# A fused attention and mixture kernel: the bias stage's pools stacked in another order

## The chip, the cores and the metric

The kernel runs on one core of one Trainium2 chip, in one launch. The metric is device time in microseconds (us): the median of repeated executions. Beside it stands one profiled execution, from which all rows below come. The engines are named as in the profile: PE (matrix multiplies), PEld (its weight loads), DVE, ACT, POOL (the three elementwise engines) and SP, which here issues every DMA (SPq is its DMA queue).

## The reference

Three layers follow each other. Attention has 4 batches, 8 heads, 576 positions of width 64, and a learned relative bias:

```python
x = (log1p(|i - j|) / log1p(max(i, 1)))[..., None]
bias = relu(x @ w1 + b1) @ w2                      # 576 x 576 x 8 heads, hidden width 32
attn = softmax(q @ k.T / 8 + bias.transpose(2, 0, 1))
x = (attn @ v)                                     # to 2304 tokens x 512
h = x @ w_in;  x = (max(h, 0) + alpha * min(h, 0)) @ w_out          # width 2048
logits = x @ phi                                   # 32 slots, 8 experts of 4
y = softmax(logits, over slots) @ experts(softmax(logits, over tokens).T @ x)
```

The bias is the same for all batches. It depends on `i` only through a scale and on `i - j`, so every row of it is a piecewise linear function.

## The kernel before, in words

**Stages.** `bias_phase` computes the bias and stores it in a DRAM tensor `W`. `Attention.run` follows, then `Moe.run` (the two dense layers and the routing) and `Experts.run`. All instructions are recorded once; a scheduler then orders each engine's instructions by a simulated timeline, apart from those that `keep_in_program_order` holds (attention from its second pair on, the late stores of the bias stage, and the preparation of the next layer's inputs among them).

**The bias stage.** For each of nine distances `k` (0 to 8) it makes 16 masks, each on DVE, ACT or POOL, in a ring of 40 (`mask`, pool `b_mask`). `unit(k, c)` multiplies masks by weights on PE into `acc` (PSUM); DVE turns `acc` into bias rows through `tmp` (L189, L190), and POOL writes their mirror image (L198) into the same tile `rows`. When a tile of rows is complete, `flush` stores it to `W` (L203, eight heads). For four of them, `rows2_2`, `rows0_2`, `rows1_3` and `rows0_3` (the number of the column block, then of the chunk), only heads 0 and 1 are stored at once; the stores of heads 2 to 7, two DMAs a tile, are put in a list `late` and issued after all else of the stage, in that order. They are the eight **late stores**, and the two of `rows0_3` are the last.

**Pools.** A tile pool is a stretch of each partition's SBUF. Pools of the left side are stacked upwards, those of `side="right"` downwards from the top, each in the order in which it is opened. The bias stage opens four on the right: `b_late` (tags b, c, d, g of the row tiles), `b_rows` (the other row tiles), `b_const` (inputs, weights, the two `tmp`) and `b_mask`. When the stage ends they are closed, and attention's and the next layer's pools grow from the left into the same bytes: `m_keep`, `m_x0`, `m_x1`, `a_z` (the scores with bias `z`, their minimum `m`, the exponentials `e`, four buffers each), `a_out`, `a_g` (four transposed tiles `g`) and `a_bias1` (the bias tile `nb` of odd head pairs). A tile waits for everything that used its bytes before, a DMA that reads them included (`reuse_waits="tile"`).

**Attention.** 16 pairs (head pair, batch) of nine tiles: `scores` (L379, PE, two PSUM buffers `s`), `shift` (L397, DVE: adds the bias `nb`, finds the minimum), `weights` (L416, ACT: exponential), `transposes` (L433, PE), `gather` (L457, one half on ACT, one on DVE, into `g`), `pv` (L472, PE). `split` (L345, L348, POOL) makes the two-part operands of a later pair. Results go to DRAM (`xT<-xo`, and the sums `rs<-rt`), and from step 8 on are loaded again (`vv<-rs`, `vv<-xT`) for the next layer's input, which DVE multiplies at L604.

**SP.** One queue, in order: an SP instruction that waits holds up all behind it. The bias tile of head pair 0, `nb`, is loaded from `W` in pieces (L310) between the last stores; behind the late stores come `early` (L622, weights of the next layer) and the `nb` of head pair 1, whose first load waits for the late stores.

Of the kernel before, what the change touches and what calls it, by code (L numbers as in the profile page):

```python
# [14 lines left out]
ALU = mybir.AluOpType  # L15
# [12 lines left out]
SLOTS = 32  # L28
# [14 lines left out]
LATE, EARLY = "bcdg", "aefmn"  # L43
# [30 lines left out]
def bias_phase(tc, ident, W, cpack, lcol, prow, xmain, xtail, att):  # L74


    nc = tc.nc
    with ExitStack() as ctx:

        def pool(name, bufs=1):  # L80
            return ctx.enter_context(tc.tile_pool(name=name, bufs=bufs, reuse_waits="tile", side="right"))

        fps = {tag: p for p, tags in ((pool("b_late"), LATE), (pool("b_rows"), EARLY)) for tag in tags}
        cp = pool("b_const")
        mp = pool("b_mask")
        ap_ = ctx.enter_context(tc.tile_pool(name="b_acc", bufs=ACC, space=PSUM, reuse_waits="tile"))

        cp_t = cp.tile([P, 14], F32, name="cp_t")
# [1039 lines left out]
def kernel(  # L1128
    ctx, tc, qk, v_l, cpack, w_l, alpha, phi, mw1, mw2, lcol, prow, xmain, xtail, scon, out
):  # L1130
    nc = tc.nc
# [5 lines left out]
    ident = const.tile([P, P], F32, name="ident")  # L1137
# [7 lines left out]
        for n, b in (("a_raw", 2), ("a_v", 3), ("a_split", 2))  # L1145
    )
    bias_phase(tc, ident, W, cpack, lcol, prow, xmain, xtail, att)

    kp = ctx.enter_context(tc.tile_pool(name="m_keep", bufs=1, reuse_waits="tile"))
    x0 = ctx.enter_context(tc.tile_pool(name="m_x0", bufs=1, reuse_waits="tile"))  # L1150
    x1 = ctx.enter_context(tc.tile_pool(name="m_x1", bufs=1, reuse_waits="tile"))
    moe = Moe(tc, ident, xT, rs, w_l, None, x0, x1)
    moe.load_alpha(alpha)
    moe.x_alloc(0)
    moe.early = x1.tile([P, 3, 1024], F32, tag="x", name="early")
    moe.idr = kp.tile([P, P], F32R, name="idr")
    nc.gpsimd.tensor_scalar(moe.idr, ident, 1.0, 1.0, ALU.mult, ALU.mult)
    moe.id4 = kp.tile([P, SLOTS], F32, name="id4")
    for k in range(4):
        q = slice(SLOTS * k, SLOTS * k + SLOTS)  # L1160
        nc.gpsimd.tensor_scalar(moe.id4[q], ident[q, q], 1.0, 1.0, ALU.mult, ALU.mult)
    set0 = att.sets[0]

    def take_stage():
# [28 lines left out]
    def at(step, f, *args):  # L1193
        extra.setdefault(step, []).append(lambda: f(*args))

    for n in range(3):
        at(3, moe.half_load, n)
    at(XONE, moe.x_alloc, 1)
# [153 lines left out]
```

## Time and profile before

| | us |
|---|---|
| median of 3 runs | 836.94 (835.46 to 837.0) |
| profiled execution | 837.26 |
| its span on the core | 835.4 |
| PE busy in the span | 772.3 (92%) |
| DVE, ACT, POOL busy | 551.8, 489.4, 332.9 |

The span is what the trace covers; 1.9 us of the execution lie around it. In the rows below a line of a timeline gives the start, the duration, engine, source line, operation, tiles written and read, the count of merged instructions, and in brackets the idle time of that engine just before and what ended it. A line of windows gives for a stretch the busy time of each engine (and instructions), the granted clock of PE as a share of full speed, the mean busy share of the DMA engines and GB/s.

### The profile page before, as it was taken

Reading aid. Unit: us, or ns where it says so; the run is one execution under the profiler, and the core shown is the slowest. Engines: PE = TensorE matmul, PEld = TensorE weight load, DVE = VectorE, ACT = ScalarE, POOL = GpSimd, SP = SyncE. Lnnn points to the kernel's source line nnn. Section 1 sums busy time; section 2 is a strip of 40 time slices with the busy share of each in tenths; the row PEclk is TensorE's granted clock in tenths of the full one; section 3 lists DMA queues with packets and bytes.
Section 4 is the critical chain, followed back from the end, with each engine's and each line's share of the span. In section 5 each row is a group of like instructions: output and inputs, shape, how many; then the busy total and the mean of one; then the engine's idle time right before and its main releaser. Section 6 shows DMA issues by size and latency. Waiting matters only on the chain.

```text
span 835.4 us, 18819 instructions
## 1 busy us (share of the span) xinstructions
PE 772.3 (92%) x7444; PEld 636.0 (76%) x7444; DVE 551.8 (66%) x1058; ACT 489.4 (59%) x1066; POOL 332.9 (40%) x423
## 2 busy tenths in 40 slices
PE   6766698999999999999999999999999999999894
PEld 5766566777767776898899888889888898988341
DVE  8766578888889886999533855575666555465202
ACT  8742467787778785434445665666566656655102
POOL 7965143555465511314312363445345233251100
PEclk9999599999999999999999999999999999999898
DMA  6799994863937211665200200050000004337996
GB/s 209 183 218 201 213 230 163 211 189 120 252 109 254 87 59 59 212 207 209 62 0 1 71 7 1 9 185 10 1 29 1 0 19 163 122 101 272 410 400 230
DMA packets 59784, 114.46 MB, mean 137 GB/s; under 512 B 10672, under 2 KB 38192, under 8 KB 57904
## 3 DMA queue, kind: packets, MB, share of 16 engines
q1 hardware_dynamic: 59696, 113.26, 44.6%
q8 instruction: 58, 0.95, 0.5%
q14 instruction: 30, 0.25, 0.1%
HBM read 91.95 MB, written 21.29 MB: 136 GB/s over the span
## 4 chain that ended last, share of the span: by engine, by line
PE 43%; DMA 4%; DVE 3%; ACT 1%; issue 1%; SPq 0%; DVEq 0%; ACTq 0%
PE ys L730 18%; PE h L697 18%; DMA ep<-in_mw_dram 2%; PE hps L1084 2%; DMA rb<-rs 1%; PE lp L789 1%; PE sp L849 0%; PE sp L848 0%; DVE vv L604 0%; DVE g L708 0%; PE tl L836 0%; DVE x L610 0%; DVE gr L718 0%; DMA vv<-xT 0%; PE tc L898 0%
## 5 line engine op out<-in xcount | busy, mean ns | idle before, releaser
L708 DVE SCALAR_TENSOR_TENSOR g<-g,nal 128x384 f32<-128x384 f32 x96 | 72.2, 752 | 77.9 <-ACT g L707 77.7
L416 ACT ACTIVATE e<-z,m 128x576 f32<-128x576 f32 x144 | 110.3, 766 | 3.8 <-DVE m L397 3.0
L397 DVE CUSTOM_DVE_ANT_0 z<-s,nb 128x576 f32<-128x576 f32 x144 | 103.3, 750 | 10.5 <-PE s L379 4.8
L716 ACT ACTIVATE gr<-g 128x384 fp32r<-128x384 f32 x95 | 49.9, 525 | 93.8 <-DVE g L708 91.6
L433 PEld LDWEIGHTS t<-ident,e 64*128 64x128 f32 x1440 | 68.3, 142 | 45.3 <-ACT g L457 12.5
L472 PE MATMUL o<-g,v 128*64 128x256 f32 (+1 forms) x640 | 94.7, 418 | 0.0
L433 PE MATMUL t<-ident,e 64*128 64x64 f32 x1440 | 81.7, 232 | 12.3 <-ACT g L457 9.6
L457 ACT ACTIVATE g<-t 128x320 f32<-128x320 f32 x144 | 62.1, 431 | 52.7 <-PE t L433 42.2
L457 DVE COPY g<-t 128x320 f32<-128x320 f32 x144 | 69.4, 485 | 28.2 <-PE t L433 23.3
L165 PE MATMUL acc<-wp,mask 128*128 128x64 bf16 (+1 forms) x1680 | 57.2, 198 | 22.4 <-issue 14.8
L705 ACT ACTIVATE g<-h 128x384 f32<-128x384 f32 x96 | 46.6, 487 | 46.4 <-PE h L697 45.8
L165 PEld LDWEIGHTS <-mask 128*128 128x128 bf16 (+1 forms) x1680 | 54.9, 103 | 24.5 <-issue 17.4
L718 DVE TENSOR_TENSOR gr<-g,gr 128x384 fp32r<-128x384 f32 x79 | 52.7, 668 | 31.1 <-ACT gr L716 29.9
L379 PE MATMUL s<-kh,qh 64*128 64x288 f32 x320 | 60.3, 346 | 7.3 <-DVE rows L190 5.4
L718 POOL TENSOR_TENSOR gr<-g,gr 128x384 fp32r<-128x384 f32 x16 | 19.3, 1207 | 117.7 <-ACT gr L716 117.7
L345 POOL TENSOR_SCALAR qh<-raw 128x608 fp32r<-128x608 f32 x32 | 21.8, 699 | 104.1 <-PE s L379 100.6
L146 ACT ACTIVATE mask<-pr,wb 128x576 bf16<-128x576 f16 (+4 forms) x81 | 47.1, 666 | 22.3 <-PE acc L165 22.2
L472 PEld LDWEIGHTS o<-g,v 128*64 128x64 f32 x640 | 41.2, 137 | 24.6 <-ACT g L457 0.5
L379 PE MATMUL s<-kl,qh 64*128 64x288 f32 x320 | 53.5, 304 | 0.0
L379 PE MATMUL s<-kh,ql 64*128 64x288 f32 x320 | 53.4, 304 | 0.0
L348 POOL TENSOR_TENSOR ql<-raw,qh 128x304 fp32r<-128x304 f32 x64 | 53.0, 860 | 0.0
L707 ACT ACTIVATE g<-h 128x384 f32<-128x384 f32 x96 | 46.6, 485 | 0.0
(1008 smaller groups left out, 2058.4 us busy)
## 6 DMA issues: line engine op xcount, KB each, us to landing
ep<-in_mw_dram SPq DMA_DIRECT2D x30, 512.0 KB
raw<-in_qk_dram SPq DMA_DIRECT2D x16, 896.0 KB
stage<-in_w_dram SPq DMA_DIRECT2D x14, 1024.0 KB
nb<-W SPq DMA_DIRECT2D x12, 576.0 KB
v<-in_v_l_dram SPq DMA_DIRECT2D x16, 320.0 KB
pre<-in_mw_dram SPq DMA_DIRECT2D x10, 512.0 KB
ex<-in_mw_dram SPq DMA_DIRECT2D x9, 512.0 KB
em<-in_mw_dram SPq DMA_DIRECT2D x8, 512.0 KB
```

Source lines behind the costliest of these rows:

```text
L165: nc.tensor.matmul(dst[:, u // 8, :, :, 4 * (u % 8) : 4 * (u % 8) + 4], mask[:, (16 * k + u) % RING, cols], wp[:, part], start=part == 0, ...
L348: self.nc.gpsimd.tensor_tensor(st[x, 1][:, c], src[:, c], st[x, 0][:, c].bitcast(F32), ALU.subtract)
L379: nc.tensor.matmul(s[:, hf, :288], st["q", a][d, o : o + P], st["k", b][d, 288 * h : 288 * h + 288], start=n_ == 0, stop=n_ == len(seq) - 1,),
L397: nc.vector.tensor_tensor_reduce(out=z.rearrange("p (a b) -> p a b", a=2), in0=s[:, :, :288], in1=self.nb[st["hp"]][:, self.SLOT[t]].rearr ...
L416: self.pin(i, nc.scalar.activation(e, z, AF.Exp, bias=m, scale=-1.0, accum_out=acc))
L433: self.pin(i, nc.tensor.transpose(tp[r][:, c], e[q, k0 : k0 + P], self.ident[q, q]))
L457: self.pin(i, nc.vector.tensor_copy(dst, src) if r else nc.scalar.activation(dst, src, AF.Copy))
L472: nc.tensor.matmul(o[64 * h : 64 * h + 64, :n], st["v"][:, h, c], g[:, c, :n], start=c == 0, stop=c == 4),
L697: nc.tensor.matmul(h, w_[:, c * P : (c + 1) * P], x_[:, c], start=c == 0 and n_ == 0, stop=c == NC - 1 and n_ == 2,)
L708: nc.vector.scalar_tensor_tensor(g, neg, self.nal[:, f : f + 1], g, ALU.mult, ALU.add)
L718: eng.tensor_tensor(gl, g, gh.bitcast(F32), ALU.subtract)
L730: i = self.nc.tensor.matmul(self.ys[blk][t], g_[:, t * P : (t + 1) * P], w_[:, 512:], start=f == 0 and n_ == 0, stop=f == NF - 1 and n_ == 2,)
```

## The change

It opens `b_const` and `b_mask` first and `b_late` and `b_rows` after them, and puts three small constants of the next layer, which were recorded right behind the bias stage, into a function that is recorded at step 16 of attention.

```diff
-        fps = {tag: p for p, tags in ((pool("b_late"), LATE), (pool("b_rows"), EARLY)) for tag in tags}
+
         cp = pool("b_const")
         mp = pool("b_mask")
+        fps = {tag: p for p, tags in ((pool("b_late"), LATE), (pool("b_rows"), EARLY)) for tag in tags}
...
-    moe.load_alpha(alpha)
     moe.x_alloc(0)
     moe.early = x1.tile([P, 3, 1024], F32, tag="x", name="early")
     moe.idr = kp.tile([P, P], F32R, name="idr")
-    nc.gpsimd.tensor_scalar(moe.idr, ident, 1.0, 1.0, ALU.mult, ALU.mult)
     moe.id4 = kp.tile([P, SLOTS], F32, name="id4")
-    for k in range(4):
-        q = slice(SLOTS * k, SLOTS * k + SLOTS)
-        nc.gpsimd.tensor_scalar(moe.id4[q], ident[q, q], 1.0, 1.0, ALU.mult, ALU.mult)
+
+    def constants():
+        moe.load_alpha(alpha)
+        nc.gpsimd.tensor_scalar(moe.idr, ident, 1.0, 1.0, ALU.mult, ALU.mult)
+        for k in range(4):
+            q = slice(SLOTS * k, SLOTS * k + SLOTS)
+            nc.gpsimd.tensor_scalar(moe.id4[q], ident[q, q], 1.0, 1.0, ALU.mult, ALU.mult)
+
...
+    at(16, constants)
```

`load_alpha` is a DMA (`nal`) and a POOL instruction that reads it. The pools' sizes follow from their tiles: `b_mask` 46,080 bytes a partition, `b_const` 17,184, `b_late` 36,864, `b_rows` 32,768. Together they take bytes 45,760 to 178,656 in both kernels. What attention's tiles lie on then is:

| tiles (bytes) | before, on | after, on |
|---|---|---|
| `m_keep`, `m_x0` (37,760 to 89,664) | `b_mask` | `b_rows`, then `b_late` |
| `early` in `m_x1` (89,664 to 101,952) | `b_mask`, `b_const` | `b_late` |
| `z` (101,952 to 111,168) | `b_const`; the last buffer also `rows3_2` | `rows0_3`; the last bytes `rows2_2` |
| `m`, `e` (111,168 to 120,512) | `rows3_2`, `rows4_2` | `rows2_2`, then `b_mask` |
| `a_out`, `a_g` (120,512 to 149,952) | `rows1_1`, `rows0_1`, `rows4_1`, `rows0_2` | `b_mask` |
| `a_bias1` (149,952 to 170,688) | `b_late` | `b_mask`, `b_const` |

The first place where instructions differ in what they wait for is DVE at the end of the bias stage. The rows give the line, the operation, what it writes and reads (with a number that tells buffers apart), the shape, and the semaphores it waits for: `DMAHW0` to `DMAHW7` count DMAs, the others are engines; `ISA` is the instruction of `shift`. Before:

```order
L190 TENSOR_TENSOR rows_3_2139<-tmp_0_2140,acc_0_2090 128x2x8x32 [waits DMAHW7_49,DMAHW1_49,Pool_49]
L190 TENSOR_TENSOR rows_3_2139<-tmp_0_2201,acc_0_2152 128x2x8x32 [waits DVE_49]
L397 ISA z_0_2292,m_0_2293<-s_0_2285,nb_1662 128x576 [waits DMAHW3_49,DMAHW6_49,DMAHW2_49,PE_49]
L397 ISA m_0_2293 128x1
L397 ISA z_1_2304,m_1_2305<-s_1_2297,nb_1662 128x576 [waits DVE_49,PE_49]
L397 ISA m_1_2305 128x1
L397 ISA z_2_2316,m_2_2317<-s_2_2309,nb_1662 128x576 [waits DMAHW5_49,DMAHW7_49,DVE_49,PE_49]
```

And after:

```order
L191 TENSOR_TENSOR rows_3_2139<-tmp_0_2140,acc_0_2090 128x2x8x32 [waits DMAHW7_49,DMAHW1_49,Pool_49]
L191 TENSOR_TENSOR rows_3_2139<-tmp_0_2201,acc_0_2152 128x2x8x32 [waits DVE_49]
L398 ISA z_0_2284,m_0_2285<-s_0_2277,nb_1662 128x576 [waits DMAHW4_49,DMAHW3_49,DMAHW5_49,DMAHW2_49,DMAHW6_49,DMAHW1_49,DMAHW7_49,PE_49,Pool_49]
L398 ISA m_0_2285 128x1
L398 ISA z_1_2296,m_1_2297<-s_1_2289,nb_1662 128x576 [waits PE_49]
L398 ISA m_1_2297 128x1
L398 ISA z_2_2308,m_2_2309<-s_2_2301,nb_1662 128x576 [waits PE_49]
```

`rows_3_2139` is `rows0_3`. In the built program the counts that the first shift waits for on `DMAHW4` and `DMAHW5` are those of the two late stores of `rows0_3`, and on `DMAHW6` and `DMAHW7` those of `rows2_2`; before, it waits for two pieces of `nb` and a store of `rows3_2`.

The second place is SP, from the last stores of heads 0 and 1 on. Before:

```order
L203 DMA W<-rows_3_1956 64x2x128
L585 DMA nal<-in_alpha_dram 128x16
L203 DMA W<-rows_2_1720 64x2x128
L310 DMA nb_1662<-W 64x2x576
L203 DMA W<-rows_2_1539 64x2x192
...
L203 DMA W<-rows_3_2139 64x6x128 x2
L622 DMA early<-in_w_dram 128x1024 x3
L310 DMA nb_3044<-W 64x4x576 x4
L310 DMA nb_3044<-W 64x576 x2
L330 DMA raw_3051<-in_qk_dram 128x1792
L484 DMA xT<-xo_0_2616 128x256
```

And after:

```order
L204 DMA W<-rows_3_1956 64x2x128
L204 DMA W<-rows_2_1720 64x2x128
L311 DMA nb_1662<-W 64x2x576 x3
L204 DMA W<-rows_2_1539 64x2x192
...
L204 DMA W<-rows_3_2139 64x6x128 x2
L311 DMA nb_3036<-W 64x576 x2
L311 DMA nb_3036<-W 64x4x576
L623 DMA early<-in_w_dram 128x1024 x3
L311 DMA nb_3036<-W 64x4x576 x3
L586 DMA nal<-in_alpha_dram 128x16
L331 DMA raw_3043<-in_qk_dram 128x1792
L485 DMA xT<-xo_0_2608 128x256
```

`nal` has moved from ahead of the late stores to behind the second bias tile; the eight late stores keep their order, and the first large load of the second bias tile now stands ahead of `early`.

On POOL `nal` stood ahead of the mirror images of `rows0_3`; now it stands behind them, right ahead of the split of pair 2. The five copies of the identity stand two mirror images earlier.

## Rows read from the trace of the kernel before

**Rows 1.** The page: busy tenths and granted clock in 40 slices of 20.9 us.

```profile
PE   6766698999999999999999999999999999999894
PEclk9999599999999999999999999999999999999898
```

**Rows 2.** Windows: busy us of each engine, PE clock, DMA share, GB/s.

```profile
80.00:90.00 10.00, 3.80 (x30) 3.13 (x32) 4.06 (x9) 2.91 (x5) 3.10 (x9) 0.59 0.86 204
90.00:100.00 10.00, 6.03 (x51) 5.45 (x49) 4.79 (x14) 3.18 (x8) 0.00 (x0) 0.50 0.99 241
100.00:110.00 10.00, 9.76 (x102) 7.37 (x104) 5.50 (x15) 6.38 (x18) 6.68 (x9) 0.72 1.03 233
110.00:120.00 10.00, 9.53 (x127) 6.54 (x124) 7.59 (x21) 6.70 (x19) 1.17 (x2) 1.00 1.06 214
130.00:140.00 10.00, 8.16 (x88) 5.87 (x88) 7.20 (x18) 5.63 (x15) 7.29 (x9) 0.83 0.59 203
```

**Rows 3.** Timeline of DVE: start, us, operation, [idle before, what ended it].

```profile
86.05 0.76 DVE L397 CUSTOM_DVE_ANT_0 z<-s,nb 128x576 f32<-128x576 f32 x1 [0.67 <-PE s L379]
...
89.55 0.76 DVE L397 CUSTOM_DVE_ANT_0 z<-s,nb 128x576 f32<-128x576 f32 x1 [2.01 <-DMA nb<-W]
...
93.74 0.76 DVE L397 CUSTOM_DVE_ANT_0 z<-s,nb 128x576 f32<-128x576 f32 x1 [2.11 <-DMA nb<-W]
...
99.61 0.49 DVE L457 COPY g<-t 128x320 f32<-128x320 f32 x1 [1.62 <-DMA W<-rows]
```

**Rows 4.** Timeline of ACT at the start of attention.

```profile
86.88 1.28 ACT L416 ACT_TABLE_LOAD   x1 [11.93 <-DVE m L397]
...
99.75 0.44 ACT L457 ACTIVATE g<-t 128x320 f32<-128x320 f32 x1 [4.01 <-DMA W<-rows]
```

**Rows 5.** Timeline of SP's DMA issues.

```profile
81.72 0.92 SPq L585 DMA_DIRECT2D nal<-in_alpha_dram  x1
82.74 0.60 SPq L203 DMA_DIRECT2D W<-rows  x1
...
84.86 0.59 SPq L310 DMA_DIRECT2D nb<-W  x1
...
91.56 7.08 SPq L203 DMA_DIRECT2D W<-rows  x8
98.69 2.23 SPq L622 DMA_DIRECT2D early<-in_w_dram  x3
104.23 4.20 SPq L310 DMA_DIRECT2D nb<-W  x6
```

**Rows 6.** Line L203, 92 to 100: durations in ns, first and last start.

```profile
L203 SPq DMA_DIRECT2D W<-rows x8: 597/798/1217, 91.6 to 98.0; - x8
```

**Rows 7.** Line L310, 101 to 104.3: SP's waits for semaphores.

```profile
L310 SPq EVENT_SEMAPHORE  x2: 28/28/28, 103.9 to 104.2; - x2
```

**Rows 8.** Timeline of PE: transposes of tiles 2 and 6, first scores of pair 2.

```profile
100.24 0.47 PE L433 MATMUL t<-ident,e 64*128 64x64 f32 x2 [2.44 <-ACT g L457]
...
107.85 0.28 PE L433 MATMUL t<-ident,e 64*128 64x64 f32 x2
...
119.94 0.38 PE L379 MATMUL s<-kh,qh 64*128 64x288 f32 x1
```

**Rows 9.** Timeline of POOL: `nal`, then the split of pair 2, first and last.

```profile
84.61 0.20 POOL L586 TENSOR_SCALAR nal<-nal 128x16 f32<-128x16 f32 x1 [2.51 <-DMA nal<-in_alpha_dram]
...
101.70 1.37 POOL L345 TENSOR_SCALAR qh<-raw 128x608 fp32r<-128x608 f32 x2 [15.63 <-PE s L379]
...
106.81 1.57 POOL L348 TENSOR_TENSOR kl<-raw,kh 128x288 fp32r<-128x288 f32 x2
```

**Rows 10.** Who SP waited for, 119 to 123: us in total, times, longest.

```profile
SPq L501 <- DMA nb<-W: 3.1, 1, 3.1
```

**Rows 11.** Timeline of SP: the last store of pair 0's sums.

```profile
122.62 0.21 SPq L501 DMA_DIRECT2D rs<-rt  x1
```

**Rows 12.** Timeline of DVE at the first input of the next layer.

```profile
133.97 0.95 DVE L604 TENSOR_TENSOR vv<-vv 128x384 f32<-128x384 f32 x1 [2.80 <-DMA vv<-xT]
```

## The prediction

> **What bounds the kernel now.** I read the page's slices first, then the windows around the place where they break, then the timelines of each engine there, and last the order in which SP issues. PE is at nine tenths from the sixth slice on [rows 1]: from there to the tail the kernel is a queue of PE work. What is late on PE where attention starts is late at the end too, unless a stall further on becomes shorter. The break lies between the bias stage and that steady part: PE is busy 3.80 of 10 us in 80 to 90, 6.03 in 90 to 100, then 9.76 and 9.53, with a granted clock of 0.59, 0.50, 0.72 and 1.00 [rows 2]. 0.50 is the lower of its two levels (1.2 GHz). The change works only here.
>
> What limits attention's start is seen on DVE and ACT. The first shift runs at 86.05, as soon as its scores are there. Two later shifts wait 2.01 and 2.11 us for pieces of the bias tile, and then both halves of a gather stop: DVE's 1.62 us, ACT's 4.01 us, until stores of rows have read the bytes that `g` gets [rows 3, 4]. From 100.24 PE goes on with the transposes of tile 2 [rows 8]. So the store of `rows0_2` ends the start of attention, but eight shifts, eight tiles of scores and two of transposes have been done before it.
>
> **The change, part by part.**
>
> *The gathers' wait goes.* `a_g` lies on masks, which were last read before attention. The 4.01 us on ACT (DVE's 1.62 lies beside it) end.
>
> *The first shift gets a wait.* `z` now lies on `rows0_3`, whose heads 2 to 7 are stored by the last two of the eight late stores, and its instruction counts on just these. Behind it on DVE stand all other shifts and the DVE halves of the gathers; ACT's table load and exponentials wait for the first minimum; PE has scores for two tiles and then no PSUM buffer; nothing of this stands ahead of the stores on SP, so it isn't a deadlock, only a later start. When do these stores land? SP issues the eight from 91.56 on, the last at 98.0 [rows 5, 6]. The first load of the second bias tile waits for them, and SP's last waits end at 103.9 and 104.2; the load follows at 104.23 [rows 5, 7]. So they have landed at 104.2 at the latest. This is the upper end. For the lower, a store issued at 82.74 had landed when a load that waits for it went out at 84.86, 2.1 us later [rows 5]: 98.0 + 2.1 = 100.1. The bounds stand 4.1 us apart. The 104.2 is a row for these very stores, in a stretch where the DMA engines are at 0.99 to 1.03 of their time [rows 2]; I take that.
>
> The Trainium skill, "DMA: Bandwidth & Descriptors", section "Anatomy of one DMA — SWDGE (gpsimd) path", gives a DMA a fixed cost of about 2.0 us, most of it the receipt of the write, and so speaks for the lower end. By it the stores would land at about 100.0, an estimate. Rows 7 disagree: the last store took some 6 us from its issue, so here a queue of packets has to be waited for. The lower end is a rival below.
>
> *`nal` leaves SP's queue ahead of the stores.* Its issue takes 0.92 us there [rows 5], and SP's issues follow each other almost without a gap, so all eight stores can move up by up to 0.92. Where they wait for the DMA engines instead it is 0. I take 0.92: the stores land at 104.2 - 0.92 = 103.3. The bounds become 99.2 and 104.2.
>
> *What the later first shift costs.* It is 103.3 - 86.05 = 17.25 us later. Before, the way from the first shift to the transposes of tile 6, where both kernels have about the same scores behind them, took 107.85 - 86.05 = 21.8 us [rows 3, 8]. Of these, 2.01 + 2.11 + 4.01 = 8.13 us are waits for DMAs that are all older than the last late store, so they are not met again: 13.67 us remain. PE runs at half clock at the start of this way in either kernel. Cost: 17.25 - 8.13 = 9.1 us. The bounds: with all three waits recovered and the early landing 99.2 - 86.05 - 8.13 = 5.0; with the latest landing and only half of the waits on the path 18.15 - 4.07 = 14.1. 9.1 is the row-by-row value, and I take it.
>
> *`nal` now stands on POOL ahead of the split of pair 2, and on SP behind the second bias tile.* With the stores at 103.3 it is issued about 5 us later (four bias loads at 4.20 / 6 = 0.7, three loads of `early` in 2.23) [rows 5], near 108.5. If it lands 2.9 us behind that, as before (81.72 to 84.61) [rows 5, 9], nothing waits, for the split's own release comes at 101.70 + 9.1 = 110.8. If it lands behind the bias tile, which before arrived only by 122.6 [rows 10, 11], the split runs from about 123 and takes 6.7 us (101.70 to 108.38) [rows 9], to 129.7. Pair 2's scores want it at 119.94 + 9.1 = 129.0 [rows 8]. Cost: 0 to 1; nearest is the row of the bias tile, ahead of `nal` in the same queue: 0.6.
>
> *A stall further on.* At 131.17 DVE waits 2.80 us for the first input of the next layer; in 130 to 140 PE is busy 8.16 us at a clock of 0.83 [rows 2, 12]: 1.84 us idle and, at 10 x 0.17, about 1.7 us lost to the clock, 3.5 in all. That load waits for stores that SP could issue only when the second bias tile had landed (122.62). With compute 9 us later and the transfers not, this could go. But `raw` of a later pair, ahead of those stores on SP, waits for the split: with the split ending at 129.7, SP's last sum store leaves some two us behind that, near 132 instead of 122.6, and the stall stays. Gain: 0 to 3.5; since I took the late split, 1.0.
>
> *Without a price.* Copies of the identity (0.30 and 1.03 us on POOL) run in an idle stretch before a mirror image; `early` lands later, but its reader moves with attention by more. PE's clock stays at 0.50 while it waits; it was there already [rows 2].
>
> The sum: 9.1 + 0.6 - 1.0 = 8.7 us, against the profiled execution of 837.26 (span 835.4, 1.9 around it): 846.0. The profiled one is 0.3 above the median, so 845.6 for the median.
>
> **The rivals.**
>
> *The late stores land early and the later stall goes.* They land at 99.2, the cost is 5.0, `nal` is early too and 3.5 come back: +1.5, or 838.5. For it: the row of 2.1 us, and in the new order `early` isn't issued until they have landed, so it can't share the DMA engines with them. Against it: the stores themselves are in a queue that is full from 91 on.
>
> *The start takes longer.* All engines begin from an empty pipeline at once, and only half the old waits were on the path: 14.1 + 0.6 = 14.7 us, or 851.6. For it: ACT needs its table (1.28 us) and four exponentials before the first gather [rows 4]. Against it: the same was so before.
>
> *Not slower.* The place is again the landing of the two stores of `rows0_3`. The change pays if the first shift starts before 86.05 + 8.13 = 94.2, or before 97.7 with the 3.5 us of the later stall. Were they landed at 95, it would be 8.95 - 8.13 - 3.5 = -2.7, or 834.2. For that SP would have to issue them three to five us sooner, and 0.92 is all that has left its queue.
>
> *The change doesn't do what it says, or the wait isn't one.* It does put `g` on masks; that `z` comes to lie on a row tile in the course of being stored is the opposite of its words. If the first shift started at 86.05 after all, only the gathers' 4.01 us would go: 833. The counts that it waits for speak against it.
>
> **How the numbers follow.** The forecast 845.6 has 0.64, the early landing 0.15, the longer start 0.12, the early stores 0.05, no wait 0.04. The range, 839.5 to 851.0, leaves out the last two, most of the early landing's lower half and the outer part of the longer start. The likeliest case alone spans 842 to 849. This kernel's measurement can't tell less than 0.2%, 1.7 us, from no change; only the early landing reaches there, with about 0.06. So faster 0.07, same 0.06, slower 0.87.
>
> **What would show it.** In the profile after: the first shift starts at 99 to 104.2 with its idle time put down to a DMA of `W<-rows`, some 13 to 18 us; ACT's and DVE's gathers show no wait for stores; PE has a gap of over 12 us behind the first two tiles of scores; the transposes of tile 6 come near 117, and from there on all is shifted by the same. `nal` on POOL waits for its DMA, and the split of pair 2 starts behind it. The forecast is wrong if the first shift still runs near 86, if the way from it to tile 6 is far from 13.7 us, or if the stall near 131 is gone and gives back three us.

## The result and the profile after

| | us |
|---|---|
| median after | 845.08 (843.71 to 847.94, 4 runs) |
| median before, on the same chip | 836.2 (834.46 to 837.0, 4 runs) |
| ratio after to before | 1.0113, 95% interval 1.0078 to 1.0149 |
| profiled execution after | 846.36, span 844.6 |

The change makes the kernel slower by about 1.1%. The forecast was 845.6, with a range of 839.5 to 851.0.

The page's slices after. The fifth digit of PE, 83.6 to 104.5 us, answers to the 6 in [rows 1]:

```profile
PE   6975199999999999999999999999999999999893
PEclk9988599999999999999999999999999999999898
```

The same stretches as in [rows 2], after (busy us of PE, PEld, DVE, ACT, POOL with counts, clock, DMA share, GB/s):

```profile
80.00:90.00 10.00, 1.81 (x12) 1.49 (x12) 1.28 (x2) 0.00 (x0) 1.22 (x2) 0.60 0.72 167
90.00:100.00 10.00, 0.00 (x0) 0.00 (x0) 0.00 (x0) 0.00 (x0) 0.00 (x0) 0.50 1.10 257
100.00:110.00 10.00, 6.36 (x67) 5.87 (x69) 5.45 (x15) 6.29 (x14) 0.00 (x0) 0.54 0.83 213
110.00:120.00 10.00, 9.68 (x128) 7.11 (x124) 7.51 (x20) 6.99 (x20) 0.00 (x0) 1.00 0.99 219
120.00:130.00 10.00, 9.54 (x126) 6.57 (x123) 7.91 (x22) 6.87 (x19) 8.61 (x13) 1.00 0.12 15
130.00:140.00 10.00, 9.41 (x137) 7.19 (x136) 9.27 (x26) 8.49 (x26) 5.09 (x7) 1.00 0.48 165
```

From 90 to 100 no engine does anything, while the DMA engines are full (share 1.10). In 130 to 140, on the other hand, PE has 9.41 us at full clock, where it had 8.16 at 0.83.

DVE after, answering to [rows 3] and [rows 12]; the first line is the bias stage's last row products:

```profile
82.37 1.28 DVE L191 TENSOR_TENSOR rows<-tmp,acc 128x512 f32<-128x512 f32 x2 [3.28 <-DMA W<-rows]
102.40 0.76 DVE L398 CUSTOM_DVE_ANT_0 z<-s,nb 128x576 f32<-128x576 f32 x1 [18.75 <-DMA nb<-W]
...
141.80 0.60 DVE L605 TENSOR_TENSOR vv<-vv 128x384 f32<-128x384 f32 x1 [1.74 <-DMA vv<-xT]
```

The first shift waits 18.75 us. The trace names a load of `nb`, the last of several semaphores to move; SP's own rows tell what was really last. SP's issues after, answering to [rows 5]:

```profile
90.39 6.99 SPq L204 DMA_DIRECT2D W<-rows  x8
97.49 5.00 SPq L311 DMA_DIRECT2D nb<-W  x3
102.59 1.69 SPq L623 DMA_DIRECT2D early<-in_w_dram  x3
104.33 1.95 SPq L311 DMA_DIRECT2D nb<-W  x3
106.32 0.60 SPq L586 DMA_DIRECT2D nal<-in_alpha_dram  x1
...
128.45 0.33 SPq L331 DMA_DIRECT2D raw<-in_qk_dram  x1
```

The stores' line in 84 to 98, answering to [rows 6] (durations in ns, first and last start):

```profile
L204 SPq DMA_DIRECT2D W<-rows x12: 574/623/1352, 84.0 to 96.7; - x12
```

SP's waits ahead of the second bias tile's loads, answering to [rows 7]:

```profile
L311 SPq EVENT_SEMAPHORE  x2: 28/28/28, 97.4 to 101.8; - x2
```

SP waits in the middle of these loads, until 101.8, for the same stores as DVE. 0.6 us later the first shift runs. The last late store was issued at 96.7, so it took 5.1 us to count as landed; before it was at most 104.2 - 98.0 = 6.2. The Trainium skill, "DMA: Bandwidth & Descriptors", section "Anatomy of one DMA — SWDGE (gpsimd) path", gives a DMA a fixed cost of about 2.0 us, and gives it for DMAs that POOL issues. These stores are issued by SP, with the DMA engines at 0.99 of their time before and 1.10 after, and the trace shows over twice that figure both times.

ACT after, answering to [rows 4]. The gather comes without a wait:

```profile
103.24 1.28 ACT L417 ACT_TABLE_LOAD   x1 [31.22 <-DVE m L398]
...
107.58 0.73 ACT L458 ACTIVATE g<-t 128x320 f32<-128x320 f32 x2
```

PE after, answering to [rows 8]: the first work behind the two tiles of scores, and the transposes of tile 6:

```profile
103.22 0.61 PE L380 MATMUL s<-kh,qh 64*128 64x288 f32 x2 [18.21 <-DVE m L398]
...
116.63 0.77 PE L434 MATMUL t<-ident,e 64*128 64x64 f32 x15
```

POOL after, answering to [rows 9]. `nal` arrives 15 us after its issue, and the split of pair 2 stands right behind it:

```profile
121.39 0.20 POOL L587 TENSOR_SCALAR nal<-nal 128x16 f32<-128x16 f32 x1 [37.03 <-DMA nal<-in_alpha_dram]
121.56 1.36 POOL L346 TENSOR_SCALAR qh<-raw 128x608 fp32r<-128x608 f32 x2
...
126.86 1.56 POOL L349 TENSOR_TENSOR kl<-raw,kh 128x288 fp32r<-128x288 f32 x2
```

### The profile page after: what moved, and what is told of

Its sections match the earlier page's. It is cut to its first block, busy times and chain, and to the rows that moved or that the text cites. A ratio compares the mean times of both kernels' runs of the same rounds, so it can differ in the third digit from the quotient of the medians.

```text
span 844.6 us, 18812 instructions
## 1 busy us (share of the span) xinstructions
PE 772.8 (92%) x7444; PEld 636.2 (75%) x7444; DVE 550.5 (65%) x1058; ACT 488.8 (58%) x1066; POOL 333.6 (40%) x423
## 4 chain that ended last, share of the span: by engine, by line
PE 41%; DMA 5%; DVE 3%; ACT 1%; issue 1%; SPq 0%; DVEq 0%; ACTq 0%
PE ys L731 18%; PE h L698 18%; DMA ep<-in_mw_dram 4%; DMA rb<-rs 1%; PE lp L790 1%; PE hps L1085 1%; PE sp L850 0%; PE sp L849 0%; DVE g L709 0%; DVE vv L605 0%; PE tl L837 0%; DVE x L611 0%; DVE gr L719 0%; DMA vv<-xT 0%; PE turn L1064 0%
## 5 line engine op out<-in xcount | busy, mean ns | idle before, releaser
L398 DVE CUSTOM_DVE_ANT_0 z<-s,nb 128x576 f32<-128x576 f32 x144 | 103.3, 750 | 26.0 <-DMA nb<-W 18.7
L434 PEld LDWEIGHTS t<-ident,e 64*128 64x128 f32 x1440 | 66.6, 140 | 40.2 <-ACT g L458 9.5
L434 PE MATMUL t<-ident,e 64*128 64x64 f32 x1440 | 79.8, 230 | 8.3 <-ACT g L458 6.7
L166 PE MATMUL acc<-wp,mask 128*128 128x64 bf16 (+1 forms) x1680 | 59.5, 201 | 18.1 <-DVE rows L191 7.1
L706 ACT ACTIVATE g<-h 128x384 f32<-128x384 f32 x96 | 46.7, 487 | 46.7 <-PE h L698 46.2
L166 PEld LDWEIGHTS <-mask 128*128 128x128 bf16 (+1 forms) x1680 | 57.3, 105 | 20.2 <-issue 7.2
L380 PEld LDWEIGHTS s<-kh,qh 64*128 64x128 f32 x320 | 35.7, 195 | 25.6 <-DVE m L398 19.9
```

The lines of the kernel that those rows point to most:

```text
L166: nc.tensor.matmul(dst[:, u // 8, :, :, 4 * (u % 8) : 4 * (u % 8) + 4], mask[:, (16 * k + u) % RING, cols], wp[:, part], start=part == 0, ...
L380: nc.tensor.matmul(s[:, hf, :288], st["q", a][d, o : o + P], st["k", b][d, 288 * h : 288 * h + 288], start=n_ == 0, stop=n_ == len(seq) - 1,),
L398: nc.vector.tensor_tensor_reduce(out=z.rearrange("p (a b) -> p a b", a=2), in0=s[:, :, :288], in1=self.nb[st["hp"]][:, self.SLOT[t]].rearr ...
L434: self.pin(i, nc.tensor.transpose(tp[r][:, c], e[q, k0 : k0 + P], self.ident[q, q]))
```

## The experiments

The theory (A): the loss is the first shift's wait for the late stores of `rows0_3`, because `z` lies on that tile; what this wait absorbs (the old gathers' wait and two waits for bias pieces) comes off it. The main rival (B): the late `nal`, and with it the late split, makes the loss. Two more came up on the way: that the constants' place in the program costs by itself (C), and that the stall near 125 to 131 is the traffic of the second bias tile (E). Some expectations name smaller rivals by a letter (D, F, and in one of them another C) and say there what they mean. Two numbers order the runs: the first shift's start, and the way from there to the end of the span. Each ratio is to runs of the kernel before made beside that row's own, so rows of different sets of runs are compared by their ratios rather than by their medians.

| kernel | median us | ratio (95%) | first shift | span | way |
|---|---|---|---|---|---|
| before | 836.2 | 1 | 86.05 | 835.4 | 749.4 |
| before, second profile | 836.82 (one run) | | 84.75 | 834.9 | 750.2 |
| changed | 845.08 | 1.0113 (1.0078 to 1.0149) | 102.40 | 844.6 | 742.2 |
| changed, second time | 847.38 | 1.0104 (1.0075 to 1.0133) | 102.61 | 843.9 | 741.3 |
| `nal` at start | 848.86 | 1.0148 (1.0125 to 1.0171) | 104.40 | 847.6 | 743.2 |
| other store order | 846.32 | 1.0125 (1.0104 to 1.0146) | 97.71 | 843.8 | 746.1 |
| both of these | 844.49 | 1.0068 (1.0041 to 1.0096) | 101.02 | 843.9 | 742.9 |
| `b_rows` opened before `b_late` | 837.61 | 1.0015 (0.9998 to 1.0033) | 84.62 | 834.0 | 749.4 |
| another stacking, `nal` at start | 838.03 | 1.0032 (1.0013 to 1.0051) | 85.13 | 835.0 | 749.9 |
| the same, second bias tile later | 833.22 | 0.9939 (0.9915 to 0.9964) | 85.42 | 829.4 | 744.0 |
| before, second bias tile later | 835.54 | 0.9972 (0.9952 to 0.9992) | 85.23 | 834.7 | 749.5 |
| constants late alone | 836.87 | 0.9993 (0.9974 to 1.0013) | 84.81 | 833.6 | 748.8 |

Where the start waits for stores, the way is 741 to 743 us, where it doesn't, 749 to 750 us; the two exceptions, 746.1 and 744.0, are explained below. The difference, 7.2 us between the first two profiles of the kernels before and after, is a little less than the 8.13 us of the prediction.

**`nal` loaded at the start of the program** (changed kernel otherwise; the identity's copies go back to their old place).

```diff
         att.load(0)
+        att.load_alpha()
...
-    at(16, constants)
```

> The changed stacking of the pools, but nal is loaded and negated at the very start of the kernel into a tile of its own, and the identity's copies are recorded where they were before the change; so nothing of the moved constants is left. Theory A (the time follows the first shift, which waits for the last two late stores): the first shift still starts at 101 to 103, the way from it to the transposes of tile 6 is still about 14 us; the split of pair 2 comes at 112 to 114 instead of 121.6 and the later stall on the next layer's first input goes, so 1 to 2.5 us less than the changed kernel, 842.5 to 844, still 6 to 8 us above the kernel before. Rival B (the loss is the moved nal, which holds POOL for 37 us and SP behind it): the time goes back to 835 to 838.

848.86 us: neither. DVE's first shift and its later input, then POOL's split:

```profile
104.40 0.76 DVE L399 CUSTOM_DVE_ANT_0 z<-s,nb 128x576 f32<-128x576 f32 x1 [18.50 <-DMA nb<-W]
...
141.62 0.55 DVE L601 TENSOR_TENSOR vv<-vv 128x384 f32<-128x384 f32 x1
```
```profile
114.60 1.36 POOL L347 TENSOR_SCALAR qh<-raw 128x608 fp32r<-128x608 f32 x2 [28.00 <-PE s L381]
```

The split now runs at 114.60 and the wait at `vv` is gone, and the way is 743.2, not shorter than 742.2. So the late `nal` costs nothing in the changed kernel: PE's queue covers it. B falls, and so do the few us that I had expected here. The first shift came 2.0 us later: the stores were issued from 92.49 on and not from 90.39, and the bias stage's last row products had come later too (84.61, not 82.37). Why is open. With `nal` at the start this stacking has these products at 84.61 and, two runs on, 84.04; its three profiles without have them at 81.81 to 83.00.

**The late stores in another order**, those of `rows0_3` second.

```diff
-        for f in late:
-            f()
+        for n in (0, 3, 1, 2):
+            late[n]()
```

> The changed kernel with the eight late stores in another order: rows2_2, rows0_3, rows0_2, rows1_3, so that the four stores whose bytes the first shift's tiles take are the first four. Nothing else is changed, nal is as late as in the changed kernel. Theory A: the first shift comes when the fourth store has landed, 95 to 98 instead of 102.4, and the time falls by as much, 4 to 7 us, to 838 to 841. Rival B: 844 to 846, as the changed kernel. Rival C (the landing is set by the queue of packets as a whole, and completion isn't in the order of issue): first shift at 101 or later, 844 to 845.

The first shift comes 4.7 us sooner, as expected, and the time does not: 846.32 us, where 838 to 841 was expected. DVE, POOL, PE and a window of this kernel:

```profile
97.71 0.76 DVE L398 CUSTOM_DVE_ANT_0 z<-s,nb 128x576 f32<-128x576 f32 x1 [14.61 <-DMA W<-rows]
```
```profile
120.16 0.36 POOL L587 TENSOR_SCALAR nal<-nal 128x16 f32<-128x16 f32 x1 [36.36 <-DMA nal<-in_alpha_dram]
```
```profile
126.46 0.40 PE L380 MATMUL s<-kl,qh 64*128 64x288 f32 x2 [1.42 <-POOL kl L349]
```
```profile
120.00:130.00 10.00, 8.02 (x88) 5.32 (x84) 5.57 (x15) 5.38 (x15) 9.84 (x15) 0.87 0.18 46
```

Here the trace names the store itself. `nal` still lands near 120, and now PE gets to pair 2 before its split is done. It is idle for 1.98 us, 0.46 in the changed kernel, and loses 1.3 (10 x 0.13) to the clock: 2.8 of the 3.9 us by which the way is longer. The late `nal` is a second limit behind the first, free only as long as the first shift is later still.

**Both together** should then give the whole gain.

> The changed stacking with both edits of the two runs before: nal loaded at the start, and the late stores in the order rows2_2, rows0_3, rows0_2, rows1_3. In the run with the order alone the first shift came 4.7 us earlier (97.71), but PE waited for the split of pair 2, which stood behind nal, and the clock fell. Theory A (the time follows the first shift wherever nothing else holds attention): first shift at 96 to 99, no wait of the scores for a split, and 3.5 to 5.5 us less than the run with nal at the start alone. Theory E (somewhere behind the start a floor is set by transfers, and whatever the first shift gains is lost there): less than 1.5 us gained.

The ratio falls from 1.0148 (`nal` at start alone) to 1.0068; by the medians that is 4.4 us less. DVE's first shift:

```profile
101.02 0.76 DVE L399 CUSTOM_DVE_ANT_0 z<-s,nb 128x576 f32<-128x576 f32 x1 [15.70 <-DMA W<-rows]
```

It is 3.4 us sooner than with `nal` at start alone, the way is 742.9, and the span's end moves by about the same (3.7). But 96 to 99 was expected: the last row products came at 84.04, 2.2 us later than with the store order alone, and the stores with them. So against the changed kernel little is gained. The intervals of the ratios overlap (1.0068 here, 1.0113 and 1.0104 there), and from the last row products to the end it is 759.9 us against 762.2 and 760.9. One of its eight times, 1245.63 us, lies far off all others and I have no cause for it; the median of the other seven is 844.25.

**`z` off the rows in flight**: the changed kernel with `b_rows` opened before `b_late`, so that `z` lies on row tiles that are stored long before.

```diff
-        fps = {... for p, tags in ((pool("b_late"), LATE), (pool("b_rows"), EARLY)) ...}
+        fps = {... for p, tags in ((pool("b_rows"), EARLY), (pool("b_late"), LATE)) ...}
```

> The changed kernel with b_rows opened before b_late: the two pools trade places, so z, m and e lie on row tiles that were stored well before, and the late row tiles lie under the next layer's tiles. The gathers lie on masks as in the changed kernel; nal is still loaded behind the second bias tile. Theory A: first shift at 84 to 86, no wait of a gather for a store, time 832 to 838: the four us of the gathers gained, against nal on POOL (pair 2's scores wait for a split that starts near 121, up to 5 us) and one load of early now issued ahead of the last pieces of the first bias tile (up to 2 us). Rival B: no better than 842, since nal is as late.

837.61 us: the loss is gone with this one line, while `nal` is as late as in the changed kernel (122.17). DVE and a window:

```profile
84.62 0.76 DVE L398 CUSTOM_DVE_ANT_0 z<-s,nb 128x576 f32<-128x576 f32 x1 [0.67 <-PE s L380]
...
90.55 0.76 DVE L398 CUSTOM_DVE_ANT_0 z<-s,nb 128x576 f32<-128x576 f32 x1 [4.44 <-DMA nb<-W]
```
```profile
120.00:130.00 10.00, 7.83 (x106) 6.47 (x104) 8.07 (x21) 6.63 (x20) 7.31 (x10) 0.83 0.48 151
```

But it isn't faster than before either, though no gather waits for a store. One piece of the bias now costs 4.44 us (SP issues a load of `early` at 80.28, ahead of it), as much as the two waits of 2.01 and 2.11 before. The stall that the kernel before had in 130 to 140 has moved to 120 to 130, where PE idles 2.17 us and loses 1.7 (10 x 0.17) to the clock. The first shift of pair 2 is 3.4 us ahead of the kernel before (117.43, 120.79), the last shift of attention 3.0 (313.74, 316.79), the end of the span 1.4: more than half of the lead is lost behind attention, as the last experiment takes up. In this kernel the split of pair 2 stands ahead of `nal` on POOL (99.98), so it says nothing about the late split.

**Another stacking** (opened in the order `b_mask`, `b_rows`, `b_late`, `b_const`) with `nal` at the start: `z` and `g` lie on rows stored early and on masks, and neither nor `nal` waits for late stores.

```diff
-        cp = pool("b_const")
         mp = pool("b_mask")
-        fps = {... (pool("b_late"), LATE), (pool("b_rows"), EARLY) ...}
+        fps = {... (pool("b_rows"), EARLY), (pool("b_late"), LATE) ...}
+        cp = pool("b_const")
```

> Pools opened in the order b_mask, b_rows, b_late, b_const, with nal loaded at the start: z, m, e on row tiles stored early, the gathers on early row tiles and masks, the late row tiles under early and the next layer's input, so that the loads of early stay behind the late stores. Theory A: first shift at 84 to 86, no store waits in a gather, the split of pair 2 near 98; from there on 3 to 6 us ahead of the kernel before, less if PE at half clock or the pieces of the first bias tile (the two waits of 2 us) set the pace: 830 to 835. Rival B: 835 to 838, as the kernel before, since the constants are early in both. Rival D (the start is bound by the half clock and the bias pieces, the gathers' wait is hidden): no change within 0.2%.

838.03 us, a miss: not better than before, although PE goes at full clock from 100 on. ACT, the waits of SP in 106 to 142 (total, times, longest) and a window near 125:

```profile
124.95 0.38 ACT L483 ACTIVATE xo<-o 128x256 f32<-128x256 f32 x1 [3.75 <-DMA xT<-xo]
```
```profile
SPq L597 <- DMA rs<-rt: 4.8, 1, 4.8
...
SPq L501 <- DMA early<-in_w_dram: 3.6, 2, 2.3
...
SPq L597 <- DMA nb<-W: 2.7, 1, 2.7
```
```profile
120.00:130.00 10.00, 6.14 (x80) 5.16 (x80) 5.46 (x15) 5.02 (x16) 1.11 (x2) 0.83 0.55 164
```

The output tile `xo` isn't free: its earlier store has been issued behind the loads of `early` and of the second bias tile, and SP itself waits for those loads ahead of small stores and reloads. PE idles 3.86 us and loses 1.7 to the clock, 5.6 in all. That is what theory E says; the next run tests it.

**The same, with the second bias tile held in program order**, behind pair 1's scores.

```diff
-            if hp == 0 and s < 4:
+            if hp == 1 or hp == 0 and s < 4:
                 self.tc.keep_in_program_order(i)
```

> The stacking b_mask, b_rows, b_late, b_const with nal at the start, and in addition the second bias tile's six loads are held in program order, so that SP issues them behind the sums of pair 1 and not right behind early. Theory E: the early start of attention was lost near 125 since the stores of results and the loads of the next layer's first input stood behind the 2.65 MB of the second bias tile in the transfers; without these, result stores land within 3 us, no ACT wait for a store of xT, the loads vv come near 118, and the gain of the start stays: 829 to 833. Rival F (the gathers' wait was worth nothing for another reason, and the wait near 125 only shows it): 836 to 838 as without the edit. A new wait is possible where the second bias tile is first used, near 155.

833.22 us, a hair above the 829 to 833 expected, and below the kernel before and the changed one; by the ratios it is 0.9% less than without the hold (1.0032, 0.9939). SP, and the same window:

```profile
102.42 1.37 SPq L618 DMA_DIRECT2D early<-in_w_dram  x3
...
112.76 1.13 SPq L597 DMA_DIRECT2D vv<-rs  x2
...
122.72 5.18 SPq L311 DMA_DIRECT2D nb<-W  x6
```
```profile
120.00:130.00 10.00, 9.37 (x140) 7.05 (x136) 8.98 (x23) 7.86 (x22) 4.14 (x6) 1.00 0.92 239
```

The six loads leave at 122.72 and not from 98.11 on, the sums are loaded again at 112.76 and not at 124.02, and PE has 9.37 us of the stretch at full clock: 3.23 less idle and 1.7 less lost to the clock, 4.9 of the 5.9 us by which the way is now shorter (744.0).

**The same hold in the kernel before**, alone.

> The kernel before with the same hold on the second bias tile's loads and nothing else. Theory E: the 2.80 us that DVE waits for the next layer's first input and PE's stall and half clock behind it (up to 3.5 us) go; the start of attention stays as it is, with the gathers' wait of 4 us: 833 to 835.5. Rival F: 836 to 837. Between this and the run with the other stacking lies what the gathers' wait is worth when nothing hides it: 2 to 4 us by theory A.

835.54 us, a small gain (the ratio's interval ends at 0.9992) at the edge of the 833 to 835.5 expected. ACT's gather and a window:

```profile
101.13 0.44 ACT L457 ACTIVATE g<-t 128x320 f32<-128x320 f32 x1 [6.30 <-DMA W<-rows]
```
```profile
130.00:140.00 10.00, 9.68 (x135) 6.93 (x133) 8.98 (x22) 7.09 (x21) 6.78 (x9) 1.00 1.05 233
```

The stall of [rows 12] is gone, the gathers' wait is not. An early start alone gave 1.0032 of before, the hold alone 0.9972, the two together 0.9939: each takes away one of two limits that lie behind each other.

**The changed kernel again**, to see how far one kernel moves.

> The changed kernel as it is, once more, beside the others of this batch and with a second profile: 843 to 848. The bias stage ended (last product with the last row tile, DVE) at 84.09 in the profile before and 82.37 in the profile after, with the same instructions in the same order; if that is the spread of single executions, this profile's end falls anywhere from 81.5 to 85, and the distance from there to the end of the span is 761 to 764.

847.38 us, last row products at 83.00, first shift at 102.61, from the products to the end 760.9, a tenth below the 761 to 764 expected (844.6 - 82.37 = 762.2 in the first profile). DVE:

```profile
102.61 0.76 DVE L398 CUSTOM_DVE_ANT_0 z<-s,nb 128x576 f32<-128x576 f32 x1 [18.32 <-DMA nb<-W]
```

**The constants' new place alone**, with the pools stacked as before.

```diff
-    moe.load_alpha(alpha)
...
+    at(16, constants)
```

> The kernel before with the second part of the change alone: the pools are stacked as before, the three constants (nal among them) are recorded at step 16 of attention. Theory A (the loss of the change is the first shift's wait for the late stores, and the constants cost next to nothing): first shift at 84 to 87, the gathers of tile 2 still wait for stores, nal lands behind the second bias tile near 120; 834 to 839 us, a ratio of 0.997 to 1.003. The split of pair 2 then has to follow nal near 120, where pair 2's scores want it at 120: up to 3 us if it is behind nal on POOL. Theory C (the constants' later place is a part of the loss): 841 to 846 us, first shift no later than 87. Whether the bias stage's last row products start earlier (82 to 83 rather than 84) when nal is not loaded inside the stage is an open question that this run also answers.

836.87 us against 836.92: nothing, so C falls. But my expectation was wrong in one point. SP and ACT:

```profile
80.55 0.92 SPq L586 DMA_DIRECT2D nal<-in_alpha_dram  x1
```
```profile
98.41 0.44 ACT L458 ACTIVATE g<-t 128x320 f32<-128x320 f32 x1 [3.96 <-DMA W<-rows]
```

Recorded at step 16, `nal` is issued at 80.55 all the same: its bytes are masks there, free early, and the scheduler draws it forward. In the changed kernel its tile lies on rows in flight, and it goes out at 106.32. So the late `nal` too is the new stacking's doing.

**The kernel before again**, a profile.

> The kernel before, unchanged, once more with a profile, to see how far its own stages move from one profiled execution to the next. Expected: span 833 to 837, first shift 85 to 87, from the first shift to the span's end 748 to 751, last row products of the bias stage at 83 to 85. If these products start before 82.5 here, the differences of 2 to 3 us in that place between kernels mean nothing.

ACT's gather and DVE's later input:

```profile
100.65 0.44 ACT L457 ACTIVATE g<-t 128x320 f32<-128x320 f32 x1 [6.09 <-DMA W<-rows]
```
```profile
133.77 0.74 DVE L604 TENSOR_TENSOR vv<-vv 128x384 f32<-128x384 f32 x1 [2.38 <-DMA vv<-xT]
```

The last row products stand at 82.79, in the first profile at 84.09: 1.3 us of difference in this place mean nothing. The gathers waited 6.09 us here and 4.01 in [rows 4], since the start was earlier and the landing later.

The clock differs too. First this profile in 130 to 140, to be held against [rows 2], then one more stretch, of the first profile and of this one:

```profile
130.00:140.00 10.00, 8.79 (x115) 6.00 (x114) 7.62 (x21) 6.33 (x17) 7.25 (x9) 1.00 0.61 197
```
```profile
235.00:245.00 10.00, 8.55 (x128) 6.63 (x128) 7.90 (x24) 8.49 (x23) 6.25 (x9) 1.00 0.53 170
```
```profile
235.00:245.00 10.00, 8.55 (x112) 6.79 (x110) 8.15 (x22) 8.22 (x22) 4.49 (x7) 0.84 0.39 128
```

The stall near 131, 3.5 us in the first profile, costs PE 1.21 us here, with no loss by the clock. In 235 to 245 PE idles 1.45 us in both, and the clock stays at 1.00 in one and falls to 0.84 in the other. So a loss by the clock of 1.6 to 1.7 us behind a short stall comes or stays away in one and the same kernel, and every sum above that counts such a loss holds for its own profile only.

Last, the part behind attention. The last shift and the first product of the output, before and after:

```profile
316.79 0.75 DVE L397 CUSTOM_DVE_ANT_0 z<-s,nb 128x576 f32<-128x576 f32 x1
...
819.51 5.24 PE L1119 MATMUL o<-st,cT 128*128 128x512 f32 x18 [1.47 <-DVE st L1114]
```
```profile
324.79 0.75 DVE L398 CUSTOM_DVE_ANT_0 z<-s,nb 128x576 f32<-128x576 f32 x1
...
828.12 5.24 PE L1120 MATMUL o<-st,cT 128*128 128x512 f32 x18 [1.47 <-DVE st L1115]
```

From the last shift to the end of the span the four profiles with the old stacking take 518.3 to 520.1 us, the eight with another one 519.8 to 522.6. From the first product of the output to the end it is 15.9 us in all four and 16.3 to 16.5 in all eight, whether their first shift is early or late. So a part of the loss, some 0.5 us and perhaps up to 2, goes with the stacking and not with the first shift. What makes it no run shows.

## Why the prediction was right, step by step

*The gathers' wait goes*: it did (107.58, no wait).

*The first shift waits for the stores of `rows0_3`*: shown. It starts at 102.40 and 102.61, where 103.3 was forecast; SP's wait for the same stores ends at 101.8. With other rows under `z` the first shift is at 84.62 again; with these stores second in line, at 97.71. The upper bound of the landing was the right row to take, and the 2.1 us of the lower one were not met again. That 0.92 of it comes from `nal`'s issue can't be told: the stores go out from 91.56 and 90.56 on before, from 90.39 and 90.99 on after.

*What the later start costs*: 16.35 us later (17.25 forecast), and the way from there to the transposes of tile 6 is 116.63 - 102.40 = 14.23 us (13.67 forecast). At tile 6 the kernel is 116.63 - 107.85 = 8.8 us late, 9.1 forecast. So of the 8.13 us of old waits 21.80 - 14.23 = 7.6 are swallowed by tile 6, not quite all, and the table's ways of 749.4 and 742.2 differ by 7.2.

*`nal` and the split of pair 2*: the late landing was right (121.39, some 123 forecast). The 0.6 us were not: the split came in time, and with `nal` at the start nothing was gained. The price is there, but only for an earlier start (about 3 us with the other store order).

*The stall near 131*: DVE's wait stayed and was smaller, as forecast (1.74 us instead of 2.80), with SP's sum stores leaving only behind the split (129.35 on). At `vv` the kernel is 141.80 - 133.97 = 7.8 us late, so 1.0 of the 8.8 has come back there, the size taken. By the first shift of pair 4 (151.49, 157.63) it is 6.1 late, so 2.6 have; in the second pair of profiles it is 9.3 late at tile 6 (108.24, 117.51) and 8.2 there (149.72, 157.90). The term was sized on a stall of 3.5 us, of which 1.7 were a loss by the clock that the kernel before doesn't have each time.

*From there all is shifted by the same*: not quite. At the last shift of attention the kernel is 8.0 us late (7.0 in the second pair), at the end 844.6 - 835.4 = 9.2 (843.9 - 834.9 = 9.0). The ups and downs inside attention are of the size of one loss by the clock. Behind attention 1.2 and 2.0 us are added, where the old stacking itself spreads over 1.8. The half us of this that lies behind the first product of the output is there with every other stacking, also where the first shift is early. The sum has no term for it.

So the first term is right in mechanism and size, 8.8 and 9.3 us for 9.1. The split cost 0 for 0.6 forecast, the stall gave back 2.6 and 1.1 for 1.0, and 1 to 2 us behind attention were not in the sum. That the total, 846.36 against 846.0, is closer than these is partly luck.

Of the rivals, the early landing and the early stores failed on when the stores landed, the longer start on the 14.23 us.

## What to carry to other kernels

A pool's place in the stack decides which transfers the next stage's first instruction waits for: put what is needed first on bytes whose last reader is long done, and what is needed late on bytes still being stored. Price a later start by the waits it swallows: here 16.4 us of delay cost about 9, because the waits that it met before were for older transfers of the same queue. And the other way round, an earlier start gains little while large loads that nobody needs yet stand ahead of small transfers that somebody does: here those loads had to be held back as well (833.22 us).

## What was not expected of the hardware

With the DMA engines full (share 0.99 and 1.10) a store took 5 to 6 us from its issue to its landing (98.0 to 104.2 at most before, 96.7 to 101.8 after). A load of 8 KB (`nal`) took 15 us (106.32 to 121.39) behind 1.57 MB of weights (128 x 3 x 1024 x 4 bytes) and 2.65 MB of bias (2 x 576 x 576 x 4 bytes), and 2.9 us when it was issued ahead of the late stores (81.72 to 84.61, [rows 5, 9]). Behind the same idle time of PE, 1.45 us, the granted clock fell to 0.84 in one profile of the kernel before and stayed at 1.00 in another. Within one kernel, the end of the bias stage moved by 1.3 us between two profiled executions, so that differences of this size between two traces had to be confirmed further on.
